# A fused RWKV and ELU-MLP kernel: the state's product with the receptance runs in two row halves into two PSUM banks, under a new order table

## The chip, the cores and the metric

The kernel runs on one core of a Trainium2 chip. The metric is the device time of one execution in microseconds (us); less is better. Beside it stands the span, which the profile measures from the first to the last instruction of the program. Engines go by the names of the profile: PE (TensorE), PEld (its weight loads), DVE (VectorE), ACT (ScalarE), POOL (GpSimd), SP (the engine that issues most transfers).

## The reference

Batch 4, 8 heads, 768 positions, head size 48; then 3072 tokens of 384 features through an MLP of 2048 hidden units, all float32.

```python
state = zeros(B, H, D, D)
for t in range(S):
    kt, vt, rt, wt = k[:, :, t], v[:, :, t], r[:, :, t], w[:, :, t]
    cur = einsum('bhd,bhe->bhde', u[None] * kt, vt)
    y[:, :, t] = einsum('bhd,bhde->bhe', rt, state + cur)
    state = wt[..., None] * state + einsum('bhd,bhe->bhde', kt, vt)
x = y.transpose(0, 2, 1, 3).reshape(B * S, H * D)
h = x @ w_in
g = where(h > 0, h, exp(minimum(h, 0)) - 1)
out = g @ w_out
```

## The kernel before

**Units and stages.** The sequence is cut into 6 chunks of 128 positions; a chunk of one batch entry is a unit, 24 units in all, numbered 0 to 23 (unit i is chunk i // 4, batch entry i % 4). Heads go in four pairs: the even head of a pair lies on partitions 0 to 47, the odd one on 64 to 111, so a pair takes 112 partitions. Of each unit DVE scans the decays (`es`, `gs`, lines 432 and 442), multiplies them into r and k (`rh`, `kh`, and for units 0 to 3 the product `rkc`, line 473). PE then does a few short steps: the scores `s` (lines 509 and 517, two PSUM banks, one for each row half), a transpose of k, `t` (line 535), the value step `v` (line 557), and the outer product for the next state, `u` (line 579); units 0 to 3 also have `pd` (line 478), the diagonal. DVE masks the scores into `am` (`mk`, lines 527 and 530), ACT copies the unit's result out of PSUM as the rounded part `xh` (line 563), and DVE the rest `xl` (line 572). ACT also checks each unit's decays (`fl`, line 458).

**The value step** `v` writes the unit's 384 features by 128 positions as three blocks of 128 partitions. From the second chunk on it first adds the state: 12 products of all 112 rows with 32 columns, then 16 products of the masked scores with the values, also of 32 columns. Four products that go to four different column strips of 32 run side by side. All float32 products are two passes on PE, so 12 products are 24 records of the profile.

**The MLP.** For each chunk (512 columns: four units) and each of the 16 parts f of the hidden layer PE does `g1` (line 268, nine matmuls: three blocks, each with the high and low parts of weights and inputs), ACT and DVE the ELU (`r1`, `r2`, `gh` on ACT; `stt`, `gl` on DVE), and PE `g2` (line 324, nine more). The first five parts for the first two units run in plain float32 from `xf` (lines 274 and 299, 256 columns). The weights arrive in 16 parts and are converted once on ACT and DVE (`a`, `cc`, `wh`, `wl`: lines 614, 622, 626, 630) during the first chunk.

**What sets the order.** Each engine follows a hand-given line of the table `ORDER`; the program is emitted in that order, and an engine waits where data or a buffer is late. The attention's PE steps share one pool of three PSUM banks (`pa`), handed out in turn: `s` takes two, `pd`, `t`, `u` and `v` one each. A step waits until the steps that held its banks before are copied out. `warm` (line 412) is ten matmuls of an identity into an accumulator that nothing reads. Where several short steps stand next to each other on PE, between two MLP steps, they are called one visit below.

```python
DIAG = ["PE"] * 4 + ["POOL"] * 20
FILL = {}
SLOTS = dict(w=2, k=3, r=3, rk=2, v=4, eg=2, md=2, am=2, kt=1, pa=3, ...)
hold("pa", ("s", i), [("mk", i, 0), ("mk", i, 1)], 2)
hold("pa", ("v", i), [("xh", i), ("xl", i)] + ...)
hold("pa", ("t", i), [("kt", i)])
hold("pa", ("u", i), [("up", i)])
```

Of the kernel before, what the change touches and what calls it, by code (L numbers as in the profile page):

```python
# [8 lines left out]
F32 = mybir.dt.float32  # L9
# [7 lines left out]
ALU = mybir.AluOpType  # L17
# [35 lines left out]
def _pieces():  # L53
    res = []
    for h in range(H):
        s, e = h * D, (h + 1) * D
        while s < e:
            n = min(e, (s // P + 1) * P) - s
            src = 64 * (h % 2) + s - h * D
            res.append((src, h // 2, s // P, s % P, n))  # L60
            s += n
    return res
# [6 lines left out]
FILL = {}  # L69
# [5 lines left out]
SPLIT = (1, 2, 3)  # L75
# [12 lines left out]
    SP=(  # L88
# [13 lines left out]
    ACT=(  # L102
# [26 lines left out]
    DVE=(  # L129
# [47 lines left out]
class Plan:  # L177
# [14 lines left out]
    def order(self):  # L192
# [20 lines left out]
        while any(lines.values()):  # L213
            n = len(order)
            for e, line in lines.items():
                while line and fits(line[0]):
# [9 lines left out]
                    order.append(ts[k])  # L226
            assert len(order) > n, {e: line[:1] for e, line in lines.items()}
        return order


def value_rounds():

# [688 lines left out]
```

## Time and profile before

| | |
|---|---|
| median of three runs | 508.4 us (507.59 to 508.52) |
| the profiled execution | 509.07 us, of which the span is 507.0 us |
| PE busy | 493.5 us of the span, 97% |
| DVE, ACT, POOL busy | 332.3, 278.2, 78.3 us |

The profiled execution took 2.07 us beside its span, and 0.67 us more than the median. PE's busy time counts overlapping records once; their ends are modelled, so the pace of the starts tells more than the busy share.

### The profile page before, as it was taken

Reading aid. Unit: us, or ns where it says so; the run is one execution under the profiler, and the core shown is the slowest. Engines: PE = TensorE matmul, PEld = TensorE weight load, DVE = VectorE, ACT = ScalarE, POOL = GpSimd, SP = SyncE. Lnnn points to the kernel's source line nnn. Section 1 sums busy time; section 2 is a strip of 40 time slices with the busy share of each in tenths; the row PEclk is TensorE's granted clock in tenths of the full one; section 3 lists DMA queues with packets and bytes.
Section 4 is the critical chain, followed back from the end, with each engine's and each line's share of the span. In section 5 each row is a group of like instructions: output and inputs, shape, how many; then the busy total and the mean of one; then the engine's idle time right before and its main releaser. Section 6 shows DMA issues by size and latency. Waiting matters only on the chain.

```text
span 507.0 us, 10454 instructions
## 1 busy us (share of the span) xinstructions
PE 493.5 (97%) x4259; PEld 414.8 (82%) x4259; DVE 332.3 (66%) x536; ACT 278.2 (55%) x565; POOL 78.3 (15%) x83
## 2 busy tenths in 40 slices
PE   4999999999999999999999999999999999999995
PEld 4879987889988888888888888888888888887884
DVE  6799999997877869674765754656556554332332
ACT  4899889785555553545354524543634443644443
POOL 3000411034141244200002420104000020000000
PEclk9999999999999999999999999999999999999999
DMA  8877759343213514305012330043040100000001
GB/s 257 252 257 233 224 179 248 114 137 119 79 50 100 155 36 147 95 18 169 1 38 91 110 109 0 32 127 119 23 137 20 49 3 1 35 29 0 1 1 67
DMA packets 27748, 48.93 MB, mean 97 GB/s; under 512 B 2864, under 2 KB 10160, under 8 KB 27696
## 3 DMA queue, kind: packets, MB, share of 16 engines
q1 hardware_dynamic: 27408, 47.83, 30.4%
q8 instruction: 35, 0.57, 0.5%
q10 hardware_dynamic: 288, 0.39, 0.2%
q14 instruction: 17, 0.14, 0.1%
HBM read 43.49 MB, written 4.72 MB: 95 GB/s over the span
## 4 chain that ended last, share of the span: by engine, by line


## 5 line engine op out<-in xcount | busy, mean ns | idle before, releaser
L278 ACT ACTIVATE m<-ph 128x512 f32<-128x512 f32 (+1 forms) x103 | 57.4, 557 | 121.9 <-PE ph L268 108.5
L284 DVE SCALAR_TENSOR_TENSOR m<-m,ph 128x512 f32<-128x512 f32 (+1 forms) x103 | 65.0, 632 | 79.1 <-ACT m L281 78.8
L268 PE MATMUL ph<-xh,w_h 128*128 128x512 f32 (+1 forms) x309 | 116.6, 377 | 0.0
L324 PE MATMUL acc<-gh,w_h 128*128 128x512 f32 (+1 forms) x308 | 115.7, 376 | 0.0
L268 PE MATMUL ph<-xh,w_l 128*128 128x512 f32 (+1 forms) x309 | 114.5, 370 | 0.0
L268 PE MATMUL ph<-xl,w_h 128*128 128x512 f32 (+1 forms) x309 | 114.3, 370 | 0.0
L324 PE MATMUL acc<-gl,w_h 128*128 128x512 f32 (+1 forms) x308 | 114.1, 370 | 0.1
L324 PE MATMUL acc<-gh,w_l 128*128 128x512 f32 (+1 forms) x308 | 114.0, 370 | 0.0
L310 DVE TENSOR_TENSOR gl<-m,gh 128x512 fp32r<-128x512 f32 (+1 forms) x103 | 70.2, 682 | 55.1 <-ACT gh L306 51.4
L306 ACT CAST gh<-m 128x512 fp32r<-128x512 f32 (+1 forms) x103 | 59.3, 576 | 53.2 <-PE acc L324 27.7
L268 PEld LDWEIGHTS ph<-xh,w_h 128*128 128x128 f32 x309 | 58.2, 188 | 11.5 <-DVE m L284 1.6
L324 PEld LDWEIGHTS acc<-gh,w_h 128*128 128x128 f32 x308 | 58.0, 188 | 10.7 <-issue 0.6
L268 PEld LDWEIGHTS ph<-xh,w_l 128*128 128x128 f32 x309 | 58.2, 188 | 10.3 <-DVE w_l L630 0.3
L324 PEld LDWEIGHTS acc<-gl,w_h 128*128 128x128 f32 x308 | 58.0, 188 | 10.0 <-DVE gl L310 0.5
L324 PEld LDWEIGHTS acc<-gh,w_l 128*128 128x128 f32 x308 | 58.0, 188 | 9.9
L268 PEld LDWEIGHTS ph<-xl,w_h 128*128 128x128 f32 x309 | 58.3, 189 | 9.4
L281 ACT ACTIVATE m<-m 128x512 f32<-128x512 f32 (+1 forms) x108 | 62.6, 584 | 1.8
L496 POOL TENSOR_SCALAR_AFFINE_SELECT am<-md 128x512 f32<-128x512 f32 x32 | 25.7, 827 | 196.5 <-DVE md L468 97.5
L461 POOL TENSOR_TENSOR rk<-rk 128x384 f32<-128x384 f32 x20 | 24.9, 1246 | 143.3 <-DMA rk<-in_rk_dram 119.9
L432 DVE TENSOR_TENSOR_SCAN eg<-w,reset 112x516 f32<-112x516 f32 x24 | 32.8, 1366 | 8.2 <-ACT junk L458 6.9
L442 DVE TENSOR_TENSOR_SCAN eg<-w,reset 112x516 f32<-112x516 f32 x24 | 30.8, 1284 | 0.8
L458 ACT ACTIVATE junk<-eg,lim 112x1032 bf16<-112x1032 f32 x24 | 27.6, 1151 | 5.2 <-DVE eg L442 5.1
(82 smaller groups left out, 500.8 us busy)
## 6 DMA issues: line engine op xcount, KB each, us to landing
rk<-in_rk_dram SPq DMA_DIRECT2D x20, 384.0 KB, 3.5
v<-in_vp_dram SPq DMA_DIRECT2D x24, 256.0 KB, 4.4
w<-in_wkr_dram SPq DMA_DIRECT2D x24, 226.2 KB, 4.8
k<-in_wkr_dram SPq DMA_DIRECT2D x24, 224.0 KB, 4.4
r<-in_wkr_dram SPq DMA_DIRECT2D x24, 224.0 KB, 4.9
wrawx<-in_w_out_dram SPq DMA_DIRECT2D x10, 383.8 KB, 6.0
wrawx<-in_w_in_dram SPq DMA_DIRECT2D x10, 383.2 KB, 5.3
out_dram<-o SPq DMA_DIRECT2D x13, 256.0 KB, 3.6
```

What stands on the lines that cost most here:

```text
L268: nc.tensor.matmul(ph, w[f][:, 0, k], x_[:, k, :], start=(k == n == 0), stop=(k == NK - 1 and n == 2))
L278: act(s["m"], s["ph"], AF.Relu, scale=-1.0)
L281: act(s["m"], s["m"], AF.Exp, scale=-1.0)
L284: stt_(s["m"], s["m"], -1.0, s["ph"], ALU.add, ALU.max)
L306: nc.scalar.copy(s["gh"], s["m"])
L310: nc.vector.tensor_tensor(s["gl"], s["m"], s["gh"].bitcast(F32), ALU.subtract)
L324: nc.tensor.matmul(a_, w[f][:, 1, m], g[:, s_], start=(begin and n == 0), stop=(stop and n == 2))
L432: nc.vector.tensor_tensor_scan(out=flat(eg[:, 0]), data0=u_["w"][:, 1:W1][:, ::-1], data1=flat(reset[:, 0]), initial=0.0, op0=ALU.mult, op ...
L442: nc.vector.tensor_tensor_scan(out=flat(u_["eg"][:, 1]), data0=u_["w"][:, 0:W1 - 1], data1=flat(reset[:, 1]), initial=0.0, op0=ALU.mult, o ...
L458: act(junk, u_["eg"].rearrange("d z p t -> d (z p t)"), AF.Relu, bias=lim, accum_out=flags[:, u_["i"]:u_["i"] + 1])
L461: eng.tensor_tensor(u_["rk"][:, 0], u_["rk"][:, 0], u_["rk"][:, 1], ALU.mult)
L496: nc.gpsimd.affine_select(out=am, in_=u_["md"][:, q::2].unsqueeze(2).broadcast_to([P, NP, C]), pattern=[[0, NP], [1, C]], compare_op=ALU.i ...
```

## The change

Six edits go together.

1. From the second chunk on, the value step's state part is 8 products of 48 rows (even head: partitions 0 to 47, the first third of the pair's 96 features; odd head: 64 to 111, the last third), interleaved, and 4 products of 112 rows (the middle third, which both heads share). The odd head's third goes to a second bank, `pa_z`; `xh` and `xl` are each written by two instructions, of 256 and of 128 columns.
2. Each of the four pairs now owns one column strip. The rows of `w_in` are permuted on the host to match.
3. The value step takes two banks of the pool of three.
4. `FILL` puts identity matmuls like those of `warm` ahead of five early steps: 3 before `pd.0`, 4 before `pd.1`, 4 before `s.0`, 5 before `t.0`, 2 before `v.0`.
5. A new `ORDER` table for all engines.
6. Four more output stores are issued in two halves.

A function that runs only when a check of the decays fails (`general`) changes too; it isn't executed.

```diff
-FILL = {}
+FILL = {('pd', 0): 3, ('s', 0): 4, ('t', 0): 5, ('v', 0): 2, ('pd', 1): 4}
-SPLIT = (1, 2, 3)
+SPLIT = [(c, 2) for c in range(5)] + [(3, 0), (4, 0)]
...
     PE=(
-        "pd.0 pd.1 t.0 s.0 warm s.1 v.0 v.1 u.0 t.1 g1.0 pd.2 g1.1 g2.0 ...
+        "warm pd.0 pd.1 s.0 t.0 s.1 v.0 v.1 u.0 g1.0 g1.1 pd.2 g2.0 ...
...
     def value(u_):
         c, b, v, am, rp = (u_[n] for n in ("c", "b", "v", "am", "r"))
-        u_["py"] = py = ps_a.tile([P, NK, C], F32, tag="pa", name="pa_y")
+        u_["py"] = py = [ps_a.tile([P, NK - (c > 0), C], F32, tag="pa", name="pa_y")]
+        if c > 0:
+            py.append(ps_a.tile([P, 1, C], F32, tag="pa", name="pa_z"))
         jobs = []
+        for i, rs in ((0, slice(0, D)), (2, slice(64, 64 + D)), (1, slice(0, R2))) if c > 0 else ():
+            for p in range(NP):
+                jobs.append((i, p, st[rs, b, p, 32 * i:32 * i + 32], rp[rs, p, :]))
         if c > 0:
-            for n in range(3 * NP):
-                p, i = divmod(n, 3)
-                jobs.append((n, st[:, b, p, 32 * i:32 * i + 32], rp[:, p, :]))
-        for p, x in ROUNDS:
-            jobs.append((3 * p + (0, 1, 1, 2)[x], v[:, P * p + 32 * x:P * p + 32 * x + 32], am[x // 2][...]))
+            jobs[0:8] = [j for z in zip(jobs[0:4], jobs[4:8]) for j in z]
+        for x in range(4):
+            for p in range(NP):
+                jobs.append(((0, 1, 1, 2)[x], p, v[:, P * p + 32 * x:P * p + 32 * x + 32], am[x // 2][...]))
...
+    def parts(u_, t):
+        t = t[:, :, u_["b"] * C:(u_["b"] + 1) * C]
+        return [(t[:, 0:2], u_["py"][0]), (t[:, 2:3], u_["py"][1])] if u_["c"] else [(t, u_["py"][0])]
...
-        nc.scalar.copy(xts[c][0][:, :, b * C:(b + 1) * C], u_["py"])
+        for t, y in parts(u_, xts[c][0]):
+            nc.scalar.copy(t, y)
...
-        hold("pa", ("v", i), [("xh", i), ("xl", i)] + ...)
+        hold("pa", ("v", i), [("xh", i), ("xl", i)] + ..., 1 + (c > 0))
...
+    w_in = inputs["moe_w_in"].view(np.int64).reshape(NP, NK, 32, DFF).transpose(1, 0, 2, 3).reshape(DM, DFF)
```

**The start on SP.** Before, the first transfers that SP issues are these (k, r and w of units 0 and 1, with the small `ubd` among them, then the first weights):

```order
L426 DMA k<-in_wkr_dram 112x512
L426 DMA r<-in_wkr_dram 112x512
L426 DMA w<-in_wkr_dram 112x517
L415 DMA ubd<-in_uz_dram 112x8
L426 DMA r<-in_wkr_dram 112x512
L426 DMA k<-in_wkr_dram 112x512
L426 DMA w<-in_wkr_dram 112x517
```

Of the change, at the same place:

```order
L409 DMA w<-in_wkr_dram 112x517
L398 DMA ubd<-in_uz_dram 112x8
L409 DMA k<-in_wkr_dram 112x512
L409 DMA r<-in_wkr_dram 112x512
L409 DMA k<-in_wkr_dram 112x512
L409 DMA r<-in_wkr_dram 112x512
L409 DMA w<-in_wkr_dram 112x517
```

The w of unit 0 went from the third place to the first; on DVE its two scans now stand ahead of `rkc.0`.

**The start on PE.** Before (`pa_d` is `pd.0` and `pd.1`, the first `pa_s` is `s.0`, the second `s.1`, `acc` from `ident` is `warm`):

```order
L478 MATMUL pa_d<-ubd,rkc 128x2 x8
L535 MATMUL pa_t<-ident,k 128x112 x4
L509 MATMUL pa_s<-r,k 128x128 x8
L412 MATMUL acc_225<-ident 128x128 x10
L509 MATMUL pa_s<-r,k 128x128 x8
L557 MATMUL pa_y<-am,v 32x128 x32
```

Of the change (L395 is `warm`, L789 the matmuls of `FILL`):

```order
L395 MATMUL acc_153<-ident 128x128 x10
L789 MATMUL acc_153<-ident 128x128 x3
L461 MATMUL pa_d<-ubd,rkc 128x2 x4
L789 MATMUL acc_153<-ident 128x128 x4
L461 MATMUL pa_d<-ubd,rkc 128x2 x4
L789 MATMUL acc_153<-ident 128x128 x4
L492 MATMUL pa_s<-r,k 128x128 x8
L789 MATMUL acc_153<-ident 128x128 x5
L518 MATMUL pa_t<-ident,k 128x112 x4
L492 MATMUL pa_s<-r,k 128x128 x8
L789 MATMUL acc_153<-ident 128x128 x2
L547 MATMUL pa_y<-am,v 32x128 x32
```

`warm` left its place between `s.0` and `s.1` and stands first; 18 more identity matmuls stand between the early steps.

**A visit of the fourth chunk on PE.** Before, one visit holds `t.14`, `s.15`, `v.14`, `v.15` and `u.14`; these are its last rows:

```order
L557 MATMUL pa_y<-r,st 32x128 x12
L557 MATMUL pa_y<-am,v 32x128 x16
L557 MATMUL pa_y<-r,st 32x128 x12
L557 MATMUL pa_y<-am,v 32x128 x16
L579 MATMUL pa_u<-v,kt 48x48 x8
```

Of the change, the visit of `u.14` and `v.15`; `s.15` with `t.14`, and `v.14`, are visits of their own, three and one MLP steps ahead of it:

```order
L575 MATMUL pa_u<-v,kt 48x48 x8
L547 MATMUL pa_y<-r,st 32x128
L547 MATMUL pa_z<-r,st 32x128
L547 MATMUL pa_y<-r,st 32x128
L547 MATMUL pa_z<-r,st 32x128
L547 MATMUL pa_y<-r,st 32x128
L547 MATMUL pa_z<-r,st 32x128
L547 MATMUL pa_y<-r,st 32x128
L547 MATMUL pa_z<-r,st 32x128
L547 MATMUL pa_y<-r,st 32x128 x4
L547 MATMUL pa_y<-am,v 32x128 x12
L547 MATMUL pa_z<-am,v 32x128 x4
```

One visit became three. Counted over the table from `t.2` to the end, 26 visits with such short steps (transposes standing alone not counted) became 41.

## Rows read from the trace of the kernel before

**Rows 1.** The page's busy times: engine, busy us, share of the span, instructions.

```profile
PE 493.5 (97%) x4259; PEld 414.8 (82%) x4259; DVE 332.3 (66%) x536; ACT 278.2 (55%) x565; POOL 78.3 (15%) x83
```

**Rows 2.** Busy time by stretch: from and to in us, length, then busy us and instructions of PE, PEld, DVE, ACT and POOL, granted TensorE clock, DMA share, GB/s.

```profile
30.00:35.00 5.00, 5.00 (x38) 4.50 (x38) 4.97 (x9) 4.97 (x15) 0.00 (x0) 1.00 1.04 371
60.00:100.00 40.00, 39.97 (x335) 33.24 (x334) 38.08 (x53) 34.07 (x69) 6.45 (x4) 1.00 0.63 188
200.00:300.00 100.00, 99.91 (x951) 82.00 (x951) 66.24 (x108) 47.99 (x91) 13.02 (x15) 1.00 0.24 74
```

**Rows 3.** Timeline of PE in the MLP; start, duration, engine, line, operation. 22 matmuls of 512 columns start from the first row to the last, this one not counted.

```profile
200.00 0.39 PE L268 MATMUL ph<-xh,w_h 128*128 128x512 f32 x1
...
204.98 0.39 PE L268 MATMUL ph<-xl,w_h 128*128 128x512 f32 x1
```

**Rows 4.** Timeline of PE in the first 45 us; behind a row, the idle time before it and what ended it.

```profile
6.52 1.84 PE L478 MATMUL pa_d<-ubd,rkc 112*128 112x2 f32 x8 [6.52 <-DMA ubd<-in_uz_dram]
...
11.53 2.08 PE L509 MATMUL pa_s<-r,k 48*128 48x128 f32 x16
13.54 4.32 PE L412 MATMUL acc<-ident 128*128 128x128 f32 x20
17.79 1.16 PE L509 MATMUL pa_s<-r,k 48*128 48x128 f32 x16
...
26.99 1.56 PE L299 MATMUL acc<-m,w_g 128*128 128x256 f32 x6 [0.49 <-DVE m L294]
...
44.49 0.47 PE L268 MATMUL ph<-xh,w_h 128*128 128x256 f32 x1
```

**Rows 5.** Timeline of DVE in the first 28 us.

```profile
4.50 0.69 DVE L473 TENSOR_TENSOR rkc<-r,k 112x512 f32<-112x512 f32 x1 [2.07 <-DMA r<-in_wkr_dram]
6.26 1.23 DVE L432 TENSOR_TENSOR_SCAN eg<-w,reset 112x516 f32<-112x516 f32 x1 [1.06 <-DMA w<-in_wkr_dram]
...
18.99 1.36 DVE L527 COPY_PREDICATED am<-upper,pa_s 128x512 f32<-128x512 uint32 x2 [1.30 <-PE pa_s L509]
21.65 0.56 DVE L572 TENSOR_TENSOR xl<-pa_y,xh 128x384 fp32r<-128x384 f32 x1 [1.30 <-ACT xf L568]
...
26.52 0.42 DVE L294 SCALAR_TENSOR_TENSOR m<-ph,m 128x256 f32<-128x256 f32 x1
```

**Rows 6.** Timeline of ACT from 8 to 30 us.

```profile
8.40 0.17 ACT L482 COPY md<-pa_d 128x8 f32<-128x8 f32 x1 [6.30 <-PE pa_d L478]
...
15.64 1.15 ACT L458 ACTIVATE junk<-eg,lim 112x1032 bf16<-112x1032 f32 x1
...
20.02 0.48 ACT L563 CAST xh<-pa_y 128x384 fp32r<-128x384 f32 x1 [1.18 <-PE pa_y L557]
```

**Rows 7.** The first transfer of the program (k of unit 0, issued 0.82 us after the span's start): the time from its issue to its landing.

```profile
DMA to landing us min/median/max: 2.8/2.8/2.8
```

**Rows 8.** Timeline of PE in the visit of `t.11`, `v.12` and `u.11`: the state part of the value step, its part with the masked scores, and the outer product.

```profile
205.92 0.86 PE L557 MATMUL pa_y<-r,st 112*32 112x128 f32 x24
206.60 1.06 PE L557 MATMUL pa_y<-am,v 128*32 128x128 f32 x32
207.59 0.56 PE L579 MATMUL pa_u<-v,kt 128*48 128x48 f32 x16
```

**Rows 9.** Timeline of PE at three visits, of each the last MLP matmul ahead of it and the second one behind it: an outer product alone (in the half-width part of the MLP, 256 columns), scores with two value steps, and scores with two value steps and an outer product.

```profile
51.50 0.28 PE L268 MATMUL ph<-xh,w_l 128*128 128x256 f32 x1
...
52.43 0.28 PE L268 MATMUL ph<-xl,w_h 128*128 128x256 f32 x1
52.55 0.28 PE L268 MATMUL ph<-xh,w_l 128*128 128x256 f32 x1
...
425.22 0.39 PE L268 MATMUL ph<-xh,w_l 128*128 128x512 f32 x1
...
427.05 1.06 PE L557 MATMUL pa_y<-am,v 128*32 128x128 f32 x32
427.93 0.84 PE L557 MATMUL pa_y<-r,st 112*32 112x128 f32 x24
...
429.91 0.40 PE L324 MATMUL acc<-gl,w_h 128*128 128x512 f32 x1
...
295.59 0.39 PE L324 MATMUL acc<-gh,w_l 128*128 128x512 f32 x1
...
299.94 0.56 PE L579 MATMUL pa_u<-v,kt 128*48 128x48 f32 x16
...
300.77 0.39 PE L268 MATMUL ph<-xl,w_h 128*128 128x512 f32 x1
```

**Rows 10.** Timeline of PE at two score steps: one of 64-row halves and all 128 columns with the transpose behind it, one of four tiles of 64 rows by 64 columns with the outer product behind it.

```profile
109.97 1.16 PE L509 MATMUL pa_s<-r,k 48*128 48x128 f32 x16
111.07 0.60 PE L535 MATMUL pa_t<-ident,k 112*128 112x112 f32 x4
...
195.80 0.90 PE L517 MATMUL pa_s<-r,k 48*64 48x128 f32 x32
196.63 0.56 PE L579 MATMUL pa_u<-v,kt 128*48 128x48 f32 x16
```

**Rows 11.** Instructions that read `pa_y`: engine, operation, count, duration in ns (least, median, most), first and last start.

```profile
L563 ACT CAST xh<-pa_y x24: 458/475/486, 20.0 to 430.1; 128x384 fp32r<-128x384 f32 x24
L572 DVE TENSOR_TENSOR xl<-pa_y,xh x24: 528/550/559, 21.6 to 431.1; 128x384 fp32r<-128x384 f32 x24
```

More of the change, by code (lines that the diff above doesn't have):

```diff
@@ L55, in _pieces @@
     for h in range(H):
[L56 to L61, printed above, removed]
+        d = 0
+        while d < D:
+            w = D * (h % 2) + d
+            n = min(D - d, 32 - w % 32)
+            res.append((64 * (h % 2) + d, h // 2, w // 32, 32 * (h // 2) + w % 32, n))
+            d += n
     return res
@@ L228, in order @@
         return order
-def value_rounds():
-    left = [(p, x) for p in range(NP) for x in range(4)]
-    rows = lambda px: (3 * px[0] + (0, 1, 1, 2)[px[1]]) % 4
-    res = []
-    while left:
-        used = set()
-        for px in list(left):
-            if rows(px) not in used:
-                used.add(rows(px))
-                res.append(px)
-                left.remove(px)
-    return res
-ROUNDS = value_rounds()
 def mlp(nc, w_h, w_l, ps_acc, ps_h, ml, gp, po, dst, last=None):
@@ L545, in value @@
         c, b, v, am, rp = (u_[n] for n in ("c", "b", "v", "am", "r"))
-        u_["py"] = py = ps_a.tile([P, NK, C], F32, tag="pa", name="pa_y")
+        u_["py"] = py = [ps_a.tile([P, NK - (c > 0), C], F32, tag="pa", name="pa_y")]
+        if c > 0:
+            py.append(ps_a.tile([P, 1, C], F32, tag="pa", name="pa_z"))
         jobs = []
+        for i, rs in ((0, slice(0, D)), (2, slice(64, 64 + D)), (1, slice(0, R2))) if c > 0 else ():
+            for p in range(NP):
+                jobs.append((i, p, st[rs, b, p, 32 * i:32 * i + 32], rp[rs, p, :]))
         if c > 0:
-            for n in range(3 * NP):
-                p, i = divmod(n, 3)
-                jobs.append((n, st[:, b, p, 32 * i:32 * i + 32], rp[:, p, :]))
-        for p, x in ROUNDS:
-            jobs.append((3 * p + (0, 1, 1, 2)[x], v[:, P * p + 32 * x:P * p + 32 * x + 32], am[x // 2][:, p, ::-1 if p > 1 and c >= TURN else 1]))
-        for n, (blk, l, r) in enumerate(jobs):
-            k, j = divmod(blk, 4)
-            same = [m for m, y in enumerate(jobs) if y[0] % 4 == j]
-            nc.tensor.matmul(py[32 * j:32 * j + 32, k], l, r, start=(n == same[0]), stop=(n == same[-1]))
+            jobs[0:8] = [j for z in zip(jobs[0:4], jobs[4:8]) for j in z]
+        for x in range(4):
+            for p in range(NP):
+                jobs.append(((0, 1, 1, 2)[x], p, v[:, P * p + 32 * x:P * p + 32 * x + 32], am[x // 2][:, p, ::-1 if p > 1 and c >= TURN else 1]))
+        bank = lambda j: (j[0] // (NK - len(py) + 1), j[1])
+        for n, j in enumerate(jobs):
+            i, p, l, r = j
+            same = [m for m, y in enumerate(jobs) if bank(y) == bank(j)]
+            z = bank(j)[0]
+            nc.tensor.matmul(py[z][32 * p:32 * p + 32, i - 2 * z], l, r, start=(n == same[0]), stop=(n == same[-1]))
+    def parts(u_, t):
+        t = t[:, :, u_["b"] * C:(u_["b"] + 1) * C]
+        return [(t[:, 0:2], u_["py"][0]), (t[:, 2:3], u_["py"][1])] if u_["c"] else [(t, u_["py"][0])]
     def x_high(u_):
-        c, b = u_["c"], u_["b"]
+        c = u_["c"]
         if c not in xts:
             xts[c] = [home.tile([P, NK, N], F32R, tag=n + str(c % 2), name=n, bufs=1) for n in ("xh", "xl")]
-        nc.scalar.copy(xts[c][0][:, :, b * C:(b + 1) * C], u_["py"])
+        for t, y in parts(u_, xts[c][0]):
+            nc.scalar.copy(t, y)
     def x_full(u_):
@@ L567, in x_full @@
             xfs.append(at.tile([P, NK, N // 2 * (1 + (F32B > 0))], F32, tag="xf", name="xf", bufs=1))
-        nc.scalar.copy(xfs[0][:, :, u_["b"] * C:(u_["b"] + 1) * C], u_["py"])
+        nc.scalar.copy(xfs[0][:, :, u_["b"] * C:(u_["b"] + 1) * C], u_["py"][0])
     def x_low(u_):
-        xh, xl = (t[:, :, u_["b"] * C:(u_["b"] + 1) * C] for t in xts[u_["c"]])
-        tt(xl, u_["py"], xh.bitcast(F32), ALU.subtract)
+        for (xh, y), (xl, _) in zip(*(parts(u_, t) for t in xts[u_["c"]])):
+            tt(xl, y, xh.bitcast(F32), ALU.subtract)
     def outer(u_):
@@ L743, in rwkv_elu_kernel @@
             if c < NC - 1:
-                add(("store", c, m), "SP", lambda m=m, c=c, fns=fns: fns["store"](m, 2 if m == NK - 1 and c in SPLIT else 1), [("out", c, m)])
+                add(("store", c, m), "SP", lambda m=m, c=c, fns=fns: fns["store"](m, 2 if (c, m) in SPLIT else 1), [("out", c, m)])
         if c == 0:
@@ L760, in rwkv_elu_kernel @@
         hold("pa", ("s", i), [("mk", i, 0), ("mk", i, 1)], 2)
-        hold("pa", ("v", i), [("xh", i), ("xl", i)] + [("xf", i)] * (i < (4 if F32B else 2 if F32A else 0)))
+        hold("pa", ("v", i), [("xh", i), ("xl", i)] + [("xf", i)] * (i < (4 if F32B else 2 if F32A else 0)), 1 + (c > 0))
         hold("pa", ("t", i), [("kt", i)])
@@ L852, in general @@
                     for b in range(B):
-                        (nc.scalar if b % 2 else nc.sync).dma_start(
+                        (nc.sync, nc.scalar, nc.gpsimd, nc.gpsimd)[b].dma_start(
                             x[dst:dst + m, k, b],
@@ L906 @@
     gu = np.broadcast_to(inputs["u"].reshape(1, NP, 2, D).transpose(2, 0, 1, 3), (2, B, NP, D)).reshape(2, B * NP, D)
-    data = {"wkr": wkr, "rk": rk, "vp": vp, "u": ub, "uz": uz, "gkrw": gkrw, "gv": gv, "gu": gu, "w_in": inputs["moe_w_in"].view(np.int64), "w_out": inputs["moe_w_out"].view(np.int64)}
+    data = {"wkr": wkr, "rk": rk, "vp": vp, "u": ub, "uz": uz, "gkrw": gkrw, "gv": gv, "gu": gu, "w_in": w_in, "w_out": inputs["moe_w_out"].view(np.int64)}
     nc = bacc.Bacc("TRN2", target_bir_lowering=False, num_devices=1, dynamic_dma_scratch_size=2048)
```

170 rows, old and new, of tables (ACT, DVE, PE, POOL) are left out of this document.

## The prediction, made blind

> **What bounds the kernel now.** The busy times come first: PE is busy for 97% of the span, DVE for 66%, ACT for 55% [rows 1]. Since PE's ends are modelled, I looked next at the pace of its starts inside the MLP. 22 matmuls of 512 columns start in 204.98 - 200.00 = 4.98 us [rows 3], 0.226 us each, evenly. An MLP step of nine is 2.04 us. Whatever lies between these matmuls, or ahead of the first, is what can change. The reader is to see two different things there. From about 27 us on PE works through its table with next to no waiting (99.91 of 100 us in one stretch [rows 2]); what costs time there is only what PE itself does in the visits of short steps. Before 27 us PE waits for others: its first `g2` starts at 26.99 [rows 4], and the chain behind it runs through DVE, which waits 1.06 us for w, 1.30 for `s.1` and 1.30 for `xf` [rows 5], and ACT, which waits 6.30 us for the first `pd` and 1.18 for `v.0` [rows 6]. So I cost the start from DVE and ACT, and the rest from PE alone. DVE's 332 busy us do not bound the whole, but until 100 us it has little to spare: 38.08 of 40 us from 60 to 100 [rows 2].
>
> **The value step.** In the state part 24 records take 206.60 - 205.92 = 0.68 us [rows 8]: six rounds of four records side by side, 0.11 us each. Are two row halves really worth twice that? The score step with 64-row halves shows it: 16 records of 128 columns, two at a time, last 111.07 - 109.97 = 1.10 us with the step to the next kind included [rows 10], that is eight rounds of 0.11 and about 0.1 to 0.2 for the switch, not sixteen rounds. The change makes the 16 records of the outer thirds run eight at a time, two rounds in place of four; the middle third keeps its two. That saves 2 x 0.11 = 0.22 us a unit.
>
> It also adds a switch of the array's shape, from halves of 64 rows to all 128, inside the step. What does a switch cost? `v` to `u` is one: 207.59 - 206.60 = 0.99 us, of which eight rounds are 0.88 [rows 8], so 0.11. That a switch of rows alone, columns kept, costs as much is not shown by this row; the score step followed by the transpose is such a pair (64 rows to all, 128 columns both) and its 1.10 us leaves 1.10 - 8 x 0.11 = 0.22 at most [rows 10]. Between nothing and 0.22 I take 0.11, the nearest. The value step then gains 0.22 - 0.11 = 0.11 us, and 20 units 2.2 us.
>
> **The visits.** The second bank breaks up the visits: scores with two banks and a value step with two do not fit into three at once. From `t.2` on, 26 visits become 41. What does splitting a visit cost? `u` alone: from the last MLP matmul ahead of it to the second one behind it 52.43 - 51.50 = 0.93 us, less two half-width matmuls of 0.12 (52.55 - 52.43), is 0.69 [rows 9]. `u` added to a visit of `s v v`: (300.77 - 295.59) - (429.91 - 425.22) = 5.18 - 4.69 = 0.49 [rows 9]. The difference, 0.20, is what it costs to give a step a visit of its own; added to the inner switch of 0.11 that it replaces, entering and leaving costs 0.31. Fifteen more visits are 15 x 0.31 = 4.65 us. In return the inner switches that cost something (two value steps in a row cost none: 0.88 us from one to the next is just the eight rounds [rows 9]) fall from 27 to 18, 9 x 0.11 = 1.0. The visits lose 3.65 us. With the value step, PE's work from `t.2` on grows by 3.65 - 2.2 = 1.45 us.
>
> **The start.** The first transfer lands 2.8 us after its issue [rows 7], at 0.82 + 2.8 = 3.6 us. With w first, DVE's scans can start there, where before it began at 4.50 [rows 5]; k and r then come while it scans. If all three DVE waits vanish too, DVE is 0.9 + 1.06 + 1.30 + 1.30 = 4.5 us ahead at its first `stt` (26.52 before): the upper end. The wait for `s.1` does vanish if PE is quicker: `warm` stood between `s.0` and `s.1` for 4.3 us, and `s.1` took 1.16 us after it, where `s.0` took 2.08 ahead of it [rows 4]; PE doubled its pace within that block. With `warm` first, about 4 us of it run while DVE still waits for w, and the 18 extra matmuls keep PE at work in its waits (0.2 us each at the later pace, 3.9 in all, in a stretch where PE otherwise waits for DVE). If that cover is gone they cost these 3.9 us. ACT sets the lower end: its first op is now the decay check, 1.15 us [rows 6], moved into the wait of 6.30; with the wait of 1.18 gone it is 2.3 us ahead. ACT and DVE are then nearly full (4.97 of 5 us each from 30 to 35 [rows 2]), so PE can keep no more lead than both have. Between 2.3 and 4.5 I take 2.9, nearer to ACT's end because ACT has every step of the first five `g1` in its queue.
>
> **What costs nothing.** The copies in two parts: whole, they are 0.475 us on ACT and 0.550 on DVE [rows 11]; a second instruction can't cost more than another whole one, so at most 20 x 0.5 = 10 us on each, on engines that have 52 and 34 of 100 us free after 200 us [rows 2]. Only units 4 to 7 fall into the stretch where DVE is 95% busy: at most 4 x 0.55 = 2.2 us there, against 1.9 free. This I leave in the range. Store halves and the row permutation lie on SP and on the host; SP's loads run ahead of use, and if a split store held one back it would be by one more issue, inside the range as well. The end of the program is unchanged.
>
> **Sum.** 1.45 - 2.9 = -1.45 us against the profiled execution's 509.07, which gives 507.6. That execution stood 0.67 above the median of 508.4; on the median's scale I predict 506.9. From no change this measurement can tell about 0.2%, 1.0 us.
>
> **Rivals.**
> - *The switch inside the value step is free* (only the rows change, the four column strips stay). Then 20 x 0.11 = 2.2 us more are saved: 504.7. Against it: each other switch in these rows shows a cost. Chance 0.09.
> - *The start gains half.* ACT and DVE have so little free time until 60 us that a lead gets lost behind one late conversion, or w alone needs longer than k did. A lead of 1.45 us is eaten exactly: 508.4, no change. For it: the two queues at 4.97 of 5; against it: both also begin earlier. Chance 0.17.
> - *The two banks make PE wait* (slower). Eight two-bank steps follow the two-bank step whose banks they get by at most two MLP steps, five transposes take the bank of the outer product just ahead in the same visit: 13 places. `v.15` now comes one MLP step and `u.14` after `v.14`, 2.04 + 0.49 us, in which ACT and DVE must empty both banks: 0.475 + 0.550 whole, up to twice that in two parts, 2.05, plus whatever they are in the middle of (`stt` and `gl` among it, and what stands behind PE is the whole MLP). It fits only just. From 0.11 us a place the gain is gone, from 0.19 the kernel is slower by over 0.2%; at 0.2, 13 x 0.2 = 2.6: 509.5. Against it: before, value steps stood directly behind scores in one visit and needed the masks of the second score step, and no wait shows there [rows 9]. Chance 0.14.
> - *Issue sets a floor.* If PE could not start small matmuls faster than the rounds need, the paired rounds would not halve. The score step's 32 records take 196.63 - 195.80 = 0.83 us with its switch [rows 10], (0.83 - 0.11) / 32 = 0.0225 each, and eight at a time need 0.11 / 8 = 0.014, which no row shows sustained. If 0.0225 is the floor, the 16 records take 0.36 and not 0.22 us, and 20 x 0.14 = 2.8 us are lost: 509.7. The Trainium skill says such a thing (TensorE: Matmul & The Clock Gate, Wait — 56ns, not 53.3ns?): starts are never closer than about 25 ns; by that the 16 records would take 0.40 us and the sum would be 3.6 us higher, 510.5. The trace's 22.5 ns lie under that already. Chance 0.06.
> - *PE stays at half pace at the start.* Then up to the end of `s.1` it has `warm` (4.3), 16 fillers at 0.43, two `pd` of 1.84 and two scores of 2.08 [rows 4], 19 us, and `s.1` ends no earlier than the 18.95 of before: no lead, 1.45 us lost or more, 510.5. Against it: ten such matmuls sufficed before. Chance 0.04.
>
> **Chances and range.** My forecast holds 0.50, its own range 505.9 to 507.8 from a lead of 2.3 to 4 us; a tenth of it lies within 0.2%. Faster: 0.44 + 0.09 = 0.53. Same: 0.06 + 0.17 = 0.23. Slower: 0.14 + 0.06 + 0.04 = 0.24. The range takes in the free switch below and the bank waits above up to 0.2 us a place: 504.7 to 509.5. What is left out is the rest of the slower cases and a lead of the full 4.5 us.
>
> **What would show it.** The state part at 16 records in about 0.22 us, then a gap, then 8 in 0.22. Visits of `v` alone near 0.31 + 1.54 - 0.11 = 1.74 us between the MLP matmuls. First `g2` near 23.5 us, and `s.0` and `s.1` both near 1.16 us. No idle time of PE ahead of `v`, `s` and `t` put down to `xh`, `xl` or `st`. I am wrong if the first `g2` starts after 25.5 us, if PE's starts inside a value step are as far apart as before, or if PE waits in the visits for copies.

## The result, and the profile after

The changed kernel is slower by 0.8%: 511.1 us (median of 20 runs, 510.2 to 515.9) against 508.1 of the kernel before on the same chip (20 runs, 507.4 to 509.0), ratio 1.0077, 95% interval 1.0059 to 1.0096. I had predicted 506.9, and the range ended at 509.5. The 20 runs lie in two clumps: 14 from 510.2 to 511.9, with a mean granted clock of 0.995 to 1.000 over the run, and six from 513.0 to 515.9, with 0.987 to 0.994. The profiled run took 515.0 us with a span of 513.4, so it belongs to the upper clump and has to be read as one of these six.

The page's busy times; before in [rows 1]:

```profile
PE 502.5 (98%) x4295; PEld 413.7 (81%) x4295; DVE 335.3 (65%) x556; ACT 279.0 (54%) x585; POOL 80.4 (16%) x83
```

Busy time by stretch, columns as in [rows 2]; the eighth number is the granted TensorE clock:

```profile
5.00:10.00 5.00, 3.81 (x27) 3.62 (x27) 4.60 (x8) 2.48 (x7) 0.83 (x1) 0.85 1.04 275
10.00:15.00 5.00, 5.00 (x29) 4.78 (x30) 3.18 (x5) 4.26 (x15) 0.00 (x0) 0.50 1.04 359
15.00:20.00 5.00, 5.00 (x40) 4.53 (x38) 2.44 (x3) 1.84 (x4) 0.00 (x0) 0.63 0.84 223
100.00:200.00 100.00, 97.83 (x1091) 82.97 (x1090) 81.39 (x145) 54.35 (x128) 22.26 (x21) 1.00 0.35 102
```

The last stretch in the kernel before:

```profile
100.00:200.00 100.00, 100.00 (x1088) 86.67 (x1087) 80.01 (x141) 55.43 (x129) 33.78 (x30) 1.00 0.35 109
```

Two things stand out. From 5 to 20 us the granted clock falls, to 0.50 (1.2 GHz) from 10 to 15; and from 100 to 200 us PE is no longer packed, it lacks 2.2 us. The start of PE (timeline; before in [rows 4]; L395 is `warm`, L789 the extra matmuls, L492 the scores, L282 the first `g2`):

```profile
1.55 4.15 PE L395 MATMUL acc<-ident 128*128 128x128 f32 x20 [1.55 <-POOL ident masks.py:199]
...
7.56 1.08 PE L461 MATMUL pa_d<-ubd,rkc 112*128 112x2 f32 x8 [1.19 <-DVE rkc L456]
8.50 2.06 PE L789 MATMUL acc<-ident 128*128 128x128 f32 x8
...
13.90 2.08 PE L492 MATMUL pa_s<-r,k 48*128 48x128 f32 x16
15.91 2.50 PE L789 MATMUL acc<-ident 128*128 128x128 f32 x10
...
18.92 1.16 PE L492 MATMUL pa_s<-r,k 48*128 48x128 f32 x16
...
26.98 1.35 PE L282 MATMUL acc<-m,w_g 128*128 128x256 f32 x5
```

`warm` does run first, but behind it PE stands idle for 1.19 us until `rkc.0` is there, then the clock falls: `s.0` takes 2.08 us, and the extra matmuls, 8 records in 2.06 us, are at half pace too and in the way. The first `g2` starts at 26.98, as before: no lead in this run.

A value step alone in a visit (timeline of PE; one MLP matmul ahead of it, the second one behind it last):

```profile
178.20 0.39 PE L307 MATMUL acc<-gh,w_l 128*128 128x512 f32 x1
178.52 0.29 PE L547 MATMUL pa_y<-r,st 48*32 48x128 f32 x1
...
178.66 0.27 PE L547 MATMUL pa_y<-r,st 48*32 48x128 f32 x1
...
178.70 0.27 PE L547 MATMUL pa_z<-r,st 48*32 48x128 f32 x1
178.90 0.42 PE L547 MATMUL pa_y<-r,st 112*32 112x128 f32 x8
179.14 0.84 PE L547 MATMUL pa_y<-am,v 128*32 128x128 f32 x24
...
180.47 0.40 PE L251 MATMUL ph<-xl,w_h 128*128 128x512 f32 x1
```

The 16 half-row records do run in two rounds of eight. But from the second round at 178.66 to the first record of all rows it is 0.24 us, where a round is 0.11, and the first round behind a change of kind takes 0.135. The state part lasts 179.14 - 178.52 = 0.62 us, against 0.68 [rows 8].

What PE waited for from 20 us on (sum in us, times, longest):

```profile
PE acc L307 <- DVE gl L293: 1.2, 1, 1.2
PE pa_t L518 <- DVE st L583: 0.9, 1, 0.9
PE ph L251 <- DVE m L267: 0.3, 1, 0.3
PE ph L257 <- DVE w_g L618: 0.2, 1, 0.2
```

The first two make nearly all of the 2.2 us missing between 100 and 200. So there are three questions: what the start is worth when the clock holds, what pairing is worth, and whether these waits come from the second bank, from the table, or from something else.

### The profile page after: what moved, and what is told of

The parts are those of the page before. It is cut to its first block, busy times and chain, and to the rows that moved or that the text cites. A ratio compares the mean times of both kernels' runs of the same rounds, so it can differ in the third digit from the quotient of the medians.

```text
span 513.4 us, 10587 instructions
## 1 busy us (share of the span) xinstructions
PE 502.5 (98%) x4295; PEld 413.7 (81%) x4295; DVE 335.3 (65%) x556; ACT 279.0 (54%) x585; POOL 80.4 (16%) x83
## 4 chain that ended last, share of the span: by engine, by line
## 5 line engine op out<-in xcount | busy, mean ns | idle before, releaser
L293 DVE TENSOR_TENSOR gl<-m,gh 128x512 fp32r<-128x512 f32 (+1 forms) x103 | 68.4, 665 | 52.3 <-ACT gh L289 44.7
L513 DVE COPY_PREDICATED am<-upper,pa_s 128x512 f32<-128x512 uint32 x32 | 23.3, 738 | 15.5 <-PE pa_s L500 15.3
L415 DVE TENSOR_TENSOR_SCAN eg<-w,reset 112x516 f32<-112x516 f32 x24 | 30.6, 1276 | 1.3 <-DMA w<-in_wkr_dram 1.2
L425 DVE TENSOR_TENSOR_SCAN eg<-w,reset 112x516 f32<-112x516 f32 x24 | 29.6, 1233 | 0.8
```

What stands on the lines that cost most here:

```text
L293: nc.vector.tensor_tensor(s["gl"], s["m"], s["gh"].bitcast(F32), ALU.subtract)
L415: nc.vector.tensor_tensor_scan(out=flat(eg[:, 0]), data0=u_["w"][:, 1:W1][:, ::-1], data1=flat(reset[:, 0]), initial=0.0, op0=ALU.mult, op ...
L425: nc.vector.tensor_tensor_scan(out=flat(u_["eg"][:, 1]), data0=u_["w"][:, 0:W1 - 1], data1=flat(reset[:, 1]), initial=0.0, op0=ALU.mult, o ...
L513: nc.vector.copy_predicated(am.rearrange("t (z p) n -> t z p n", z=2), uppers, windows(pa))
```

## The experiments

All ratios are against runs of the kernel before on the same chip.

**No extra matmuls.**

```diff
-FILL = {('pd', 0): 3, ('s', 0): 4, ('t', 0): 5, ('v', 0): 2, ('pd', 1): 4}
+FILL = {}
```

> The changed kernel without the 18 extra matmuls at the start; `warm` stays first. Theory A (the extra matmuls are on the way when the clock falls): in the profile of after, the granted clock is 0.50 from 10 to 15 us, and 26 records of extra matmuls between 8.5 and 18 us start 0.207 us apart, 5.4 us in all, ahead of `s.0`, `t.0` and `s.1`. Without them PE reaches the end of `s.1` near 15 us even at half pace, the first `g2` starts between 22 and 25.5 us, and the time is 508 to 511 us with no second clump near 515. Theory B (the extra matmuls hold the clock up in most runs): without them every run has the low clock to 18 us or longer, and all runs look like the slow clump of after, 513 to 516 us.

Measured: 512.7 us (511.8 to 514.2), ratio 1.0094 (1.0077 to 1.0111). Timeline of PE at the start:

```profile
7.11 3.80 PE L461 MATMUL pa_d<-ubd,rkc 112*128 112x2 f32 x16 [0.92 <-DVE rkc L456]
10.83 2.08 PE L492 MATMUL pa_s<-r,k 48*128 48x128 f32 x16
...
23.38 0.92 PE L282 MATMUL acc<-m,w_g 128*128 128x256 f32 x3
```

Both theories were half right. In the profiled run the pace is half from `pd.0` on, yet nothing stands in the way, and the first `g2` starts at 23.38, 3.6 us earlier than before. That run is the fastest of the six, with a mean clock of 0.999; the other five have 0.984 to 0.990, as low as the upper clump of the changed kernel, and take 512.3 to 514.2 us. So without the extra matmuls the clock falls in most runs, as theory B says, but a run near 515 is no longer among them, and none is better than 511.8. The extra matmuls are useful when the clock holds and harmful when it doesn't.

**More extra matmuls, so that PE does not stand idle behind `warm`.**

```diff
-FILL = {('pd', 0): 3, ...
+FILL = {('pd', 0): 9, ...
```

> The changed kernel with 9 instead of 3 extra matmuls between `warm` and the first `pd`, which fill the 1.2 us that PE stands idle there before `pd.0` at 7.56 us. Theory A (that idle time lets the clock fall): the granted clock stays at 1.00 from 5 to 20 us, `s.0` and `s.1` both take about 1.16 us, the first `g2` starts between 23 and 25 us, and all runs lie near 510.5 us or below, none above 512. Theory B (something else lets it fall): the clock is 0.5 to 0.6 between 10 and 20 us in some of the runs as before, and the runs lie in two clumps near 510.7 and 515.

Measured: 510.8 us, all runs from 510.5 to 511.6, ratio 1.0050 (1.0035 to 1.0064). PE at the start, and the stretch from 10 to 15 us:

```profile
5.98 2.17 PE L789 MATMUL acc<-ident 128*128 128x128 f32 x18
7.99 0.95 PE L461 MATMUL pa_d<-ubd,rkc 112*128 112x2 f32 x8
...
11.65 1.16 PE L492 MATMUL pa_s<-r,k 48*128 48x128 f32 x16
...
14.44 1.54 PE L492 MATMUL pa_s<-r,k 48*128 48x128 f32 x16
...
22.83 1.35 PE L282 MATMUL acc<-m,w_g 128*128 128x256 f32 x5
```

```profile
10.00:15.00 5.00, 5.00 (x49) 4.53 (x50) 4.93 (x8) 4.97 (x16) 0.00 (x0) 1.00 1.04 353
```

Theory A held: with PE at work behind `warm` the clock stays at 1.00 in the profiled run (mean clocks of all six 0.998 or 0.999), the upper clump is gone (the two later kernels with these nine on the new table, 11 runs, have none either), and the first `g2` starts at 22.83: a lead of 26.99 - 22.83 = 4.2 us. That this kernel is still 0.5% slower than before means that more than 6 us are lost behind it. From the first `g2` to the last matmul it needs 504.00 - 22.83 = 481.2 us; the kernel before needs 501.59 - 26.99 = 474.6.

**The outer thirds unpaired, two banks kept.**

```diff
-        for i, rs in ((0, slice(0, D)), (2, slice(64, 64 + D)), (1, slice(0, R2))) if c > 0 else ():
+        for i in range(NK) if c > 0 else ():
             for p in range(NP):
-                jobs.append((i, p, st[rs, b, p, 32 * i:32 * i + 32], rp[rs, p, :]))
-        if c > 0:
-            jobs[0:8] = [j for z in zip(jobs[0:4], jobs[4:8]) for j in z]
+                jobs.append((i, p, st[:, b, p, 32 * i:32 * i + 32], rp[:, p, :]))
```

> The changed kernel with the outer thirds as products of all 112 rows again, one at a time, in the same two banks, strips and table. From the rows of after: the state part of a value step lasts 179.144 - 178.520 = 0.62 us against 0.68 in the kernel before, so the pairing is worth 0.055 us a unit and this kernel is 20 x 0.055 = 1.1 us slower than after. The prediction's own step says 0.11 a unit, 2.2 us slower; its rival of a free switch 4.4 us slower. Rival to all: same time as after, because PE waits elsewhere for what the step gained. The start is that of after, with its two clumps.

Measured: 512.1 us, ratio 1.0084 (1.0065 to 1.0102). Timeline of PE in a value step, its state part and the start of the masked part:

```profile
178.32 0.64 PE L545 MATMUL pa_y<-r,st 112*32 112x128 f32 x16
178.78 0.40 PE L545 MATMUL pa_z<-r,st 112*32 112x128 f32 x8
179.00 0.84 PE L545 MATMUL pa_y<-am,v 128*32 128x128 f32 x24
```

The state part is 0.68 us again, 0.06 more than in pairs. The 49 visits behind the first `g2`, from the last MLP matmul ahead to the second one behind and less these two at their usual pace (0.227 us of 512 columns, 0.120 of 256, 0.216 in plain float32), add up to 82.72 us here and 81.56 with pairs (kernel with nine extra matmuls): pairing is worth 1.16 us, half of what I predicted. The times alone do not show it: the ratio with pairs was 1.0077, and the two intervals overlap.

**One bank, unpaired: table and start alone.**

```diff
-        u_["py"] = py = [ps_a.tile([P, NK - (c > 0), C], F32, tag="pa", name="pa_y")]
-        if c > 0:
-            py.append(ps_a.tile([P, 1, C], F32, tag="pa", name="pa_z"))
+        u_["py"] = py = [ps_a.tile([P, NK, C], F32, tag="pa", name="pa_y")]
...
-        hold("pa", ("v", i), [...], 1 + (c > 0))
+        hold("pa", ("v", i), [...], 1)
```

> The changed kernel with the outer thirds unpaired and the whole value step in one bank, with one copy each for the high and low part: the new table and the new start alone. Theory A (the second bank makes PE wait, 1.39 us at 111.6 and 0.9 at 130.2 in after among others): the waits vanish, 2 to 3 us faster than the unpaired kernel with two banks, that is near 509.5. Theory B (the waits come with the table): as slow as the unpaired kernel, within 0.5 us.

Measured: 512.8 us, ratio 1.0093 (1.0075 to 1.0112). PE's waits:

```profile
PE acc L307 <- DVE gl L293: 1.1, 1, 1.1
PE pa_t L518 <- DVE st L579: 0.8, 1, 0.8
```

Theory B: both long waits are there with one bank. They come with the table. From the first `g2` to the last matmul this kernel takes 482.2 us, the unpaired one with two banks 482.3.

**The two long waits, DVE's order mended.** The kernel with nine extra matmuls, and in DVE's line:

```diff
-stt.20 gs.7 rh.7 kh.7 stt.21 gl.20 gl.21
+stt.20 gs.7 gl.20 rh.7 kh.7 stt.21 gl.21
-xl.7 gl.25 sc.8 up.6
+xl.7 up.6 gl.25 sc.8
```

> The changed kernel with 9 extra matmuls ahead of the first `pd`, and two moves in DVE's order: `gl.20` goes ahead of `rh.7 kh.7 stt.21`, and `up.6` ahead of `gl.25 sc.8`. Theory A (the two long waits of PE, 1.3 us for `gl` near 106 us and 0.9 us ahead of `t.7` near 126 us, are only a matter of what stands ahead of these two steps in DVE's queue): both waits go, 510.8 - 2.2 = 508.6 us. Theory B (DVE has too much to do in this stretch, and what is moved back makes PE wait next): the waits turn up a step later, 510 to 511 us.

Measured: 509.9 us, ratio 1.0039 (1.0027 to 1.0051). Both waits are gone, and one of 0.4 us for a mask (`mk`) has come:

```profile
PE pa_s L492 <- DVE am L510: 0.4, 1, 0.4
```

From the first `g2` to the last matmul it is 480.3 us, 0.9 less, not 2.2: theory B for the larger part. DVE has too much to do there. Why?

**POOL's work of one unit left out.** Beside the scan that made `gl` late, POOL was at work (kernel with nine extra matmuls; timeline of POOL, DVE and PE):

```profile
102.25 1.01 POOL L444 TENSOR_TENSOR rk<-rk 128x384 f32<-128x384 f32 x1 [11.95 <-DVE reset L424]
102.26 2.09 DVE L425 TENSOR_TENSOR_SCAN eg<-w,reset 112x516 f32<-112x516 f32 x1
...
103.34 1.80 POOL L447 TENSOR_TENSOR rk<-rk,ub 128x384 f32<-128x384 f32 x1
...
104.39 1.31 DVE L429 TENSOR_TENSOR r<-r,eg 112x512 f32<-112x512 f32 x1
...
106.82 1.51 DVE L293 TENSOR_TENSOR gl<-m,gh 128x512 fp32r<-128x512 f32 x2
...
107.55 0.50 PE L307 MATMUL acc<-gl,w_h 128*128 128x512 f32 x1 [1.27 <-DVE gl L293]
```

```diff
-        eng.tensor_tensor(u_["rk"][:, 0], u_["rk"][:, 0], u_["rk"][:, 1], ALU.mult)
+        if u_["i"] != 9:
+            eng.tensor_tensor(u_["rk"][:, 0], u_["rk"][:, 0], u_["rk"][:, 1], ALU.mult)
```

and the same for the multiplication by `ub`.

> The changed kernel with 9 extra matmuls ahead of the first `pd`, and without the two multiplications that POOL does for unit 9 (`rk.9`, `rku.9`; the diagonal term of that unit is left wrong). In the kernel with them POOL works from 102.25 to 105.1 us, and beside it DVE's scan takes 2.09 us in place of 1.23 and the multiplication behind it 1.31 in place of 0.68, 1.48 us more, right ahead of the `gl` that PE waits 1.3 us for. Theory A (POOL's work stretches DVE's, and that makes the wait): both take their usual times and the wait near 106 us goes, 509.5 us. Theory B (the order of DVE's queue alone makes it): the durations or the wait stay, 510.8 us.

Measured: 509.6 us, ratio 1.0036 (1.0023 to 1.0049). The same stretch, DVE's order unchanged:

```profile
102.25 1.23 DVE L425 TENSOR_TENSOR_SCAN eg<-w,reset 112x516 f32<-112x516 f32 x1
...
103.52 0.69 DVE L429 TENSOR_TENSOR r<-r,eg 112x512 f32<-112x512 f32 x1
...
106.11 0.45 PE L307 MATMUL acc<-gl,w_h 128*128 128x512 f32 x1
```

Theory A: the scan takes 1.23 us again, the multiplication 0.69, and PE does not wait. First `g2` to last matmul is 479.4, 1.7 us less. The table had put POOL's work beside DVE's where DVE has nothing to spare.

The wait for `st` near 127 us is still there (0.9). Ahead of it too POOL multiplies, and a multiplication of DVE is stretched (kernel with nine extra matmuls):

```profile
124.11 1.38 POOL L444 TENSOR_TENSOR rk<-rk 128x384 f32<-128x384 f32 x1 [5.86 <-DMA rk<-in_rk_dram]
...
125.57 1.07 POOL L447 TENSOR_TENSOR rk<-rk,ub 128x384 f32<-128x384 f32 x1
...
125.70 1.36 DVE L525 TENSOR_TENSOR st<-st,pc 112x384 f32<-112x384 f32 x1
```

The same instruction took 0.53 us at 122.80, with POOL idle. That POOL makes this wait as well was not tried.

**The new start on the old table.** Orders of the changed kernel up to the ninth MLP step, those of the kernel before from there on, old value step, nine extra matmuls.

> The kernel before with the start of the changed one alone: the orders of PE, ACT, DVE and SP are the new ones up to `g1.8`, `r1.8`, `stt.8` and the load of the seventh weight tile, the old ones from there on; `warm` first, and the extra matmuls (9 ahead of the first `pd`). The value step has one bank and three products of all rows, as before. Theory A (the lead of 4.2 us at the first `g2` is worth what it was lost for in the changed kernel, and the old table keeps it but for some 0.5 to 1 us of early waits): 508.5 - 3.3 = 505.2 us, between 504.3 and 505.8. Theory B (ACT and DVE are full until 60 us and eat the lead): 507 to 508.5 us.

Measured: 518.1 us, ratio 1.0203 (1.019 to 1.0217). A splice of mine spoilt it; DVE's waits:

```profile
DVE md L468 <- POOL rk L464: 11.8, 1, 11.8
```

The new head has `md.4` early, the old tail loads what it reads late. From step 13 on the steps ran 9.2 us behind the kernel before, and to within 0.15 us equally far to the end: on the old table a lead or a delay goes through.

**The same with the changed value step on top.**

> As the kernel with the new start on the old table, and the changed value step on top: outer thirds in pairs, two banks, copies in two parts. Two value steps that follow each other in one visit need four banks of three, so seven steps of ACT and DVE (`xh` or `xl` of units 10, 14, 16, 18, 21, 22, `mk.21`) are moved ahead of what stood before them, without which the order could not go on. Theory A (the two banks make PE wait where two value steps stand together): PE waits for both copies of the unit before, 0.475 + 0.550 us and up to 2 us with what is in front of them, at seven to ten places, 7 to 15 us slower than the kernel with the start alone, 512 to 520 us. Theory B (banks do not matter): 20 x 0.055 = 1.1 us faster than that kernel, near 504.

Measured: 560.6 us, ratio 1.1051 (1.1031 to 1.1072), with the same fault of the splice, so 42 us more than the kernel without the new value step. PE's waits:

```profile
PE pa_z L547 <- DVE xl L568: 18.9, 6, 6.7
...
PE pa_z L547 <- DVE am L513: 3.8, 6, 0.9
```

Theory A, and far more than I expected, 42 us against an upper end of 15. Without the wait for `gl` that both kernels of this splice have (10.0 and 10.7 us), PE waits 30.0 us behind the start. The granted clock falls as well, to 0.83 from 100 to 120 us and 0.93 from 200 to 250 and from 350 to 400, where the kernel without the new value step has 1.00 from 100 to 500; so not all of the 42 us are waits. Two banks need the new table's split visits, and these are what the second bank costs.

**The splice mended** (`md.4` back in its old place).

> The kernel with the start of the changed one on the old table, with one step put back: `md.4` in DVE's order stands where the old table has it (behind `cc.10`), since in the first splice it came ahead of the load and of POOL's multiplication that it reads, and DVE waited 11.8 us for it. From step 13 on that splice ran in the old table's time to within 0.1 us, so a lead should go through to the end. Theory A: the lead of 3.6 us that it had at the eighth MLP step is kept: 507.8 to 508.5 less 3.6, 504.2 to 505.2 us. Theory B (other loads or the two full engines eat it between 45 and 100 us): 506.5 to 508.5 us.

Measured: 507.6 us, ratio 0.9996 (0.9986 to 1.0005). The lead at the first `g2` is 4.5 us, 3.1 at step 8, 1.6 from step 13 on. Half of the lead is lost between 48 and 64 us: theory B.

**Only w first and DVE's scans first.**

```diff
-SP  ld_k.0 ld_r.0 ld_w.0 ubd ld_r.1 ld_k.1
+SP  ld_w.0 ubd ld_k.0 ld_r.0 ld_k.1 ld_r.1
-DVE rkc.0 es.0 kh.0 rkc.1 gs.0 rh.0
+DVE es.0 gs.0 rkc.0 rh.0 kh.0 rkc.1
```

> The kernel before with one part of the new start: w loaded first and DVE's two scans ahead of `rkc.0`. PE's order, with `warm` between `s.0` and `s.1`, and ACT's stay. Theory A (the lead comes from DVE beginning earlier): DVE starts at 3.8 us in place of 4.5 and no longer waits for w, `xf` comes 1 to 2 us earlier, first `g2` near 25 to 26 us, 506.5 to 507.5. Theory B (PE's half pace ahead of `warm` holds the chain, and `rkc.0`, which PE needs first, now comes 2 us later): the first `g2` at 27 us or later, 508 to 510 us.

Measured: 509.0 us, ratio 1.0017 (1.0007 to 1.0028); first `g2` at 26.82. Theory B: no lead. PE waits longer for `rkc.0`, and at half pace its chain holds everything. The two profiled spans differ by 0.2 us the other way, but the 507.0 of before is a long one: the spans of 22 of its runs here lie from 505.2 to 506.9. Why the median is 0.9 us above that of before stays open.

```profile
PE pa_d L478 <- DVE rkc L473: 7.5, 1, 7.5
```

**A scan moved out of the full stretch, and fewer extra matmuls.** In DVE's line `es.4` goes from behind `stt.8` to ahead of `gs.4`; then the same with `('pd', 0): 6`.

> The new start on the old table, with one more move in DVE's order: the first scan of unit 4 (`es.4`, 1.22 us) goes from behind `stt.8` to right ahead of its second scan `gs.4`, some 9 us later. In the kernel without this move the lead at the MLP steps falls from 3.2 us at step 8 to 1.6 us at step 13 and stays there to the end; in that stretch, 48.8 to 60 us, DVE works back to back, and beside POOL's multiplications it takes 1.77 us for a `w_l` and a `wg` in place of 0.95 each, and 0.89 twice for a `gl` in place of 0.42. Theory A (the scan stands in the way of `wl` and `stt`): the lead after step 13 is 2.5 to 2.8 us, 506.4 to 506.7 us. Theory B (POOL's work takes it from DVE whatever stands there, and the scan is missed 9 us later): lead 1.6 or less, 507.6 or more.

> The same with 6 in place of 9 extra matmuls ahead of the first `pd`. With 9 the last of them starts at 7.87 us and `pd.0` at 7.99; in the kernel with 3, `pd.0` starts at 7.22 to 7.30, when `rkc.0` is there. Six end near 7.2 us. Theory A: `pd.0` and all behind it 0.6 us earlier, clock at 1.00 throughout, 0.2 to 0.6 us faster than with 9. Theory B (the shorter cover lets the clock fall in some runs): a second clump 4 us above the others.

Measured: 507.7 us, ratio 0.9990 (0.9978 to 1.0002), theory B: the move does nothing. With six: 507.1 us, ratio 0.9979 (0.9968 to 0.9990), clock at 1.00. This version is faster than both kernels. Its lead is 3.3 us at step 12 and 1.9 at step 13.

**The same without POOL's multiplications of units 4 and 5.** DVE's scans and a `gl` with them, and then without:

```profile
54.02 1.24 DVE L310 TENSOR_TENSOR gl<-m,gh 128x256 fp32r<-128x256 f32 x1
55.18 2.04 DVE L432 TENSOR_TENSOR_SCAN eg<-w,reset 112x516 f32<-112x516 f32 x1
```

```profile
53.78 0.43 DVE L310 TENSOR_TENSOR gl<-m,gh 128x256 fp32r<-128x256 f32 x1 [0.17 <-ACT gh L306]
54.12 1.22 DVE L432 TENSOR_TENSOR_SCAN eg<-w,reset 112x516 f32<-112x516 f32 x1
```

> The new start on the old table with 6 extra matmuls (the kernel with `es.4` moved), without the four multiplications that POOL does for units 4 and 5 between 51.9 and 58 us (the diagonal term of these units is left wrong). With them the lead is 3.3 to 3.6 us at steps 9 to 12 and 1.9 at step 13. Theory A (POOL's work stretches DVE's, which has no free time there, and so eats the lead): `wg`, `w_l` and `gl` take their usual 0.95, 0.95 and 0.42 us throughout, the lead stays at 3 us or more behind step 13, and the time is 507.1 - 1.4 = 505.7 us. Theory B (DVE and ACT have too much to do there anyway): lead 2 us, 507.0.

Measured: 505.6 us, ratio 0.9950 (0.9934 to 0.9966). Theory A, to 0.1 us: the lead at step 13 is 3.7 us and stays 3.7 to 4.0 to the end. POOL's four multiplications, 5.4 us of an engine that the page shows 16% busy, cost the whole kernel 1.5.

## Why the prediction was wrong

| step | predicted, us | measured, us |
|---|---|---|
| lead at the first `g2` | -2.9 | -3.9 to -4.8 when the clock holds (new table); none in the profiled run of after |
| visits split | +3.65 | +4.0 |
| value step | -2.2 | -1.16 |
| PE's waits behind the start | 0 | +2.2 for `gl` and `st`, +0.5 in two short ones, 0.6 not placed |

Apart from the range of the lead, the measured terms are those of the kernel with nine extra matmuls against the kernel before: 6.57 us more from the first `g2` to the last matmul. Of it 0.4 is `t.1`, which now stands behind that point; the visits, 49 for 33, are 82.72 - 0.90 - 77.38 - 0.41 = 4.0 (unpaired, without PE's wait for `st`), pairing gives back 1.16. With the lead of 4.2 this makes 2.4, and the spans differ by 2.2. These are single profiled runs, and that of before is at the long end of its runs: the kernel with the mended splice ends 1.5 us ahead of it, and its median is 0.5 us below that of before.

**The visits** were right. From the last MLP matmul ahead to the second one behind, scores with a transpose take 1.84 us, scores with an outer product 1.98 and an outer product alone 0.93 in both kernels; a value step alone is 180.47 - 178.20 - 0.45 = 1.82 us, predicted 1.74, and most of the difference is the value step's. The copies in two parts cost nothing that can be seen, as predicted: one copy or two, one bank or two, differ by 0.2 us in all. The split stores were not tried alone.

**The value step: the switch was mis-sized.** The rounds are halved as I said. But the step between halves and all rows costs 0.24 - 0.11 = 0.13 us, and the first round behind it 0.025 more than the later ones; together 0.16 where I took 0.11, the nearest row. Of the 0.22 saved 0.06 is left. The bound of 0.22 that I had read from the transpose held. The Trainium skill (TensorEngine Tiling (Array Packing), Key Properties) says that a change of tiling mode drains the engine; the 0.20 us between 178.70 and 178.90, on either side of which records start 0.01 us apart, agree. The rival of an issue floor fell: eight records start within 0.05 us of each other.

**The start: right mechanism, wrong size, and one assumption that fails in some runs.** The lead was larger than 2.9 (in the kernels with the original three extra matmuls the first `g2` starts at 22.24 and 22.34). DVE's end of my bounds was the truth, not ACT's. But I wrote that the extra matmuls keep PE at work in its waits. Three of them leave 1.2 us idle ahead of `pd.0`, and in six of 20 runs the kernel is 2 to 5 us slower; all six have a lower mean clock than the other 14, and in the one that was profiled the clock fell right there. I gave the rival of half pace 0.04 and 510.5 us, from a row in which ten matmuls had sufficed; the row did not show that the pace stays. That idle time is the cause is shown as far as filling it made the upper clump go. It does not always let the clock fall (the unpaired kernel was profiled with 1.04 us idle there and the clock at 1.00), and on the old table one of 24 runs with nine extra matmuls and one of twelve with six still have a mean clock of 0.994 and lie 1.7 and 1.8 us above their medians. What sets these runs apart stays open.

**The waits: the step that failed most.** My sum had no term for PE's waits behind the start: I wrote that from 27 us on only what PE itself does costs time, and took the two banks for the only new danger, with 0.2 us at 13 places. Under the new table they were harmless, but PE waited 2.7 us for DVE; a sign that I had named, idle time ahead of a transpose for `st`, was among it. What I left out is that a new table puts every engine's work beside other work. I had read 38.08 of 40 us on DVE from 60 to 100 [rows 2], and looked at DVE's queue as a sum, not at what runs beside it. POOL's work makes DVE's longer, and where this falls on a full stretch PE waits. Shown: near 106 us by leaving POOL's work out, between 48 and 64 us on the old table in the same way. Not tried: the wait for `st`, ahead of which DVE is stretched too, and the short waits near 42 and 46 us in the kernel with nine extra matmuls, where POOL works from 39 to 45 us.

## What to carry to other kernels

A matmul that keeps the clock up is worth its place only if no idle time is left behind it; look at the spread of the runs, not at one profile. Before moving work by a table, lay POOL's rows beside DVE's, since an engine that is hardly busy can hold up one that has nothing to spare. The price of changing the array's shape inside a step is read from the start of one kind to the start of the next, and a saving of two rounds can be nearly all of it.

## What the runs showed of the hardware that I had not expected

DVE's instructions with two inputs in SBUF take up to three times as long when POOL multiplies beside them: a scan 2.09 us for 1.23, `gl` of 256 columns 1.24 for 0.43. Those with one input in PSUM keep their time: in the kernel with nine extra matmuls `xl` of 256 columns takes 0.41 to 0.43 us in 14 places without POOL's multiplications and in six beside them. The rows of unit 9 fit turns in which one holds up the other: the scan starts 0.01 us behind POOL's 1.01 us and takes 0.86 longer, POOL's next multiplication, started during the scan, takes 1.80 where the first took 1.01, and DVE's multiplication, started during that one, takes 1.31 for 0.69. The Trainium skill (SBUF — State Buffer, SBUF: two separate sides) says that the two engines share a pair of ports that one instruction holds to its end; these rows agree.

And the 1.00 that the profile prints for the clock is not a reading everywhere. The trace's clock records begin at 17.38 us in the kernel before, at 17.97 without the extra matmuls and at 5.04 in the profile of after; a stretch without a record is printed as 1.00. So `s.0` takes 2.08 us beside a printed 1.00 without extra matmuls, as it did before [rows 4], and the same 2.08 us beside a recorded 0.50 in the profile of after: at the start the pace of the matmuls tells more than the clock column.
